# Cosine attention, Fourier mix and feed-forward on one core: a planner with new durations and new step orders

## The chip, the core and the metric

The kernel runs on one core of a Trainium2 chip. Its engines work side by side, each through its own list of instructions: TensorE (PE; loading the weights of a product is shown apart, as PEld), VectorE (DVE), ScalarE (ACT), GpSimd (POOL) and SyncE (SP), which here only issues transfers. They wait for each other by semaphores. The metric is the time of one execution on the device in microseconds (us); the median of three runs is given. One further execution was taken with the hardware profiler, and all views come from it.

## What is computed

```python
q_n = q / (norm(q, axis=-1) + 1e-6);  k_n = k / (norm(k, axis=-1) + 1e-6)
attn = softmax(q_n @ k_n.T / tau)            # 8 batches, 12 heads, 448 rows, 64 wide
x = (attn @ v) as (8, 448, 768)              # the 12 heads side by side
u = x + real(fft(fft(x, axis=1), axis=2))
un = (u - mean(u)) / sqrt(var(u) + 1e-6)     # over the 768
out = u + maximum(un @ w_ch1, 0) @ w_ch2     # 768 -> 3072 -> 768
```

## The kernel before

**Work and names.** The eight batches (0 to 7) go through the same stages, and a step's name carries the batch behind the underscore: `un0_2` is block 0 of batch 2. Where one name is given to several steps, `#1` is the second of them.

- Loads (`ld_q0_4`, `ld_k0_4`: SyncE, lines 890 and 1011; `ld_v...`: GpSimd, line 1065; the weights `W1_..` and `W2_..`: GpSimd, lines 816 and 817).
- Normalizing q and k: squares on ScalarE (`sq`, L896 for batches 0 and 1, else L1020), sums on VectorE (`ss`, L899, L1022), the reciprocal norm through logarithm and exponential on ScalarE and a reciprocal on VectorE (`ln`, `nrm`, `eps`, `rcp`: L835 to L839), scaling (`sc`). For batches 0 and 1 the scaling is `scK`, `scQ` and `scT` (L918, L922) on VectorE or GpSimd, and TensorE transposes (`tk`, `tq`); from batch 2 on it is `sc0` to `sc6` (L1033, three instructions each) on GpSimd, and transposing transfers of SyncE bring the blocks into place (`tr0` to `tr6`, L1039).
- Attention: scores on TensorE (`qk`, L1112, L1125), exponentials on ScalarE (`ex`, L1089, 900 columns an instruction), the product with v (`pv`, L1143, L1149), the reciprocal sum and the scaling on VectorE (`rd`, `x`: L1167, L1169), then small sums (`f`, `fa`, `g`, `e`).
- Fourier mix: two short products on TensorE (`fs`, `fd`), sums on VectorE (`pq` L1398, `u` L1409 or L1421), and the normalization of each block of 128 rows: `ba` (VectorE, L1446), `bs`, `ln2` and `rs` (ScalarE, L1451 to L1456), `un` (VectorE, L1463), then the transpose of the normalized block into UNT: by TensorE in batch 0 (`tn`, L1472), by a SyncE transfer from batch 1 on (`tru`, L1483, from buffer F).
- Feed-forward: products with w_ch1 (`h0` to `h23`, L1548 for the first, else L1557; two blocks together where they are a pair, `#1` for the second pair of a batch), the relu on ScalarE or VectorE (`relu`, L1573), and the products with w_ch2. These are in part formed from sums of quarters (`s10`, `s50` and such: VectorE, L1805; products `y`, `m10`, `m50`: L1701), and are put together in OUTB: by VectorE (`fin`, L1738), or by a copy on ScalarE and an addition of u on GpSimd (`fa0`, L1722, and `fa0p`, L1727, two instructions). `m50_4` accumulates on after `fin00_4`, a VectorE step that adds to what `fa0p_4` left.
- Stores: `st` on SyncE (L1752), `sc_1` and such on GpSimd (L1760).

Ahead of the first feed-forward product stand tables built on the chip (cosines and sines: `iota`, `tqs`, `sins`, `sind`, `sinp`, `sinn`, the last two being sign-changed copies for the Fourier products), the table load of ScalarE for logarithm and exponential (`ldt0`, L791), and attention and Fourier mix of batch 0. TensorE fills its pauses there with products whose result isn't used (`warm`, L1965). From the first product of line 1548 (`h0_0`) on, TensorE has work of several batches interleaved: feed-forward of one batch, attention of the next.

**What sets the order.** The program is written as a list of steps (`P.add`: the engines that may take it, a function that issues it, a duration for each engine, a name, what it reads and writes). A long string, `STEPS`, gives each step its engine and its place in that engine's list: `un0_2 326d` is the 326th place on VectorE; the letters are t (TensorE), a (ScalarE), d (VectorE), p (GpSimd), s (SyncE). A step of several instructions under one name has several numbers. SyncE's places order its transfers, and GpSimd's places its arithmetic and its transfers in one list. So the order on every engine is fixed by hand or by a search, and an engine waits at the head of its list until that step's inputs are there.

`schedule()` then walks through these lists with durations from two tables, `TIMES` (for a step and engine: time to the result, time to the next step) and `FLOW` (for a transfer: latency, service, share of the bandwidth), and with durations written at the step. What comes of this walk in the program is the slot in TensorE's accumulators (two of kind M, three of kind G) that each tile takes, and with it whom a step waits for, and the places of the warm-up products (`fill`). The steps' order comes from `STEPS` alone. `emit()` writes each engine's list with its waits.

```python
if e == "sp":
    rt = max(rt, sync[-2].end - DMA_LAT if sync[-2] else 0.0)
...
if e == "pool" and op.piece:
    port.append((t, op, op.piece))
elif e == "dve" and op.port and port and port[-1][1].end > t:
    x, p, z = port[-1]
    y = x + z * math.ceil((t - x + 0.02) / z)
    if y < p.end - 0.1:
        p.end += d
        free["pool"] += d
```

The first lines hold a transfer of SyncE in the walk until the one before the last is near its end. The others model a VectorE step (one named in `PORT`: `un`, `s`, `u`, `sc`, `f`, `g`, `e` and others) that begins while a GpSimd step made of pieces runs: the VectorE step begins at a piece's end, and the GpSimd step ends later by its duration. `QUEUES` fixes the order of the first loads.

Of the kernel before, what the change touches and what calls it, by code (L numbers as in the profile page):

```python
# [90 lines left out]
scT0_0 21d, tk0_0 0t, ek0_0 12a, tq0_0 1t, eq0_0 14a, tt0_0 3t, et0_0 27d 29, ld_k1_0 6s, ld_q1_0 0s, ld_t1_0 5s, sqK1_0 15a, ssK1_0 26d, sqQ1_0 10a,
ssQ1_0 20d, sqT1_0 13a, ssT1_0 25d, scK1_0 33d, scQ1_0 34d, scT1_0 32d, scK2_0 22p, scQ2_0 35d, scT2_0 21p, tk1_0 6t, ek1_0 36d, tq1_0 7t, eq1_0 22a,
tk2_0 13t, ek2_0 45d, tq2_0 11t, eq2_0 39d, tt1_0 10t, et1_0 43d 40, ld_k2_0 8s, ld_q2_0 4s, ld_t2_0 7s, sqK2_0 21a, ssK2_0 37d, sqQ2_0 11a,
ssQ2_0 23d, sqT2_0 24a, ssT2_0 38d, scK3_0 46d, scQ3_0 26p, scT3_0 44d, scK4_0 32p, scQ4_0 31p, scT4_0 49d, scK5_0 50d, scQ5_0 53d, scT5_0 25p,
# [1931 lines left out]
```

## Time and profile before

| | us |
|---|---|
| median of 3 runs | 573.87 (573.54 to 575.36) |
| the profiled execution | 577.4 |
| its span, first to last instruction | 575.3 |
| start of the first product of `h0_0` | 47.57 |
| TensorE busy, of the span | 555.4 |

The profiled execution lies 3.5 us above the median, and 2.1 us of it lie around its span. In the views, times are microseconds from the span's start, unless ns stands with them. A row of the timeline has start, duration, engine, line, operation, result and inputs, and the number of instructions taken together; a row of the chain of waits has start, duration and what the end was waiting for at that time. "SPq" is SyncE's issuing of a transfer, "DMA UNT<-F" the transfer itself until it has landed. Mean granted clock of TensorE over the span: 0.994.

### The profile page before, as it was taken

The numbers are of one execution on the slowest core, as the hardware profiler recorded it, in microseconds if no ns is written. First come the engines' busy times: TensorE is split into PE (matmuls) and PEld (weight loads), VectorE is DVE, ScalarE is ACT, GpSimd is POOL, SyncE is SP. The second block draws the span as 40 slices with busy tenths as digits, with TensorE's granted clock in tenths as the row PEclk, the third lists the DMA queues.
The fourth block names the chain that finished last, engine by engine and source line by source line (L and its number), as shares of the span: only waits on it lengthen the run. The fifth ranks groups of instructions, "written<-read, shape, count | busy, mean of one in ns | idle before, by whom it ended". The sixth has DMA issues, their size and how long they took to land.

```text
span 575.3 us, 15949 instructions
## 1 busy us (share of the span) xinstructions
PE 555.4 (97%) x6582; PEld 435.9 (76%) x6582; DVE 428.6 (75%) x941; ACT 368.0 (64%) x710; POOL 232.9 (40%) x346
## 2 busy tenths in 40 slices
PE   3999999999999799999999999899999999999997
PEld 2778887685786688868878788587786886969694
DVE  6989778876588468876789578876687499896362
ACT  6898885465876486787538776575566642747150
POOL 6663422367445424563471446530553103031203
PEclk9999999999999799999999999999999999999999
DMA  9999987949569936953594549634565310022011
GB/s 204 187 241 184 182 148 97 174 102 181 143 79 104 186 70 113 111 116 112 105 124 110 107 98 137 111 83 98 84 118 43 70 16 26 33 42 71 2 57 56
DMA packets 187897, 62.19 MB, mean 108 GB/s; under 512 B 166800, under 2 KB 185616, under 8 KB 187824
## 3 DMA queue, kind: packets, MB, share of 16 engines
q1 hardware_dynamic: 129856, 38.35, 35.3%
q0 software_dynamic: 57968, 22.81, 31.2%
q8 instruction: 52, 0.85, 0.6%
q14 instruction: 21, 0.17, 0.1%
HBM read 51.90 MB, written 11.01 MB: 109 GB/s over the span
## 4 chain that ended last, share of the span: by engine, by line
PE 84%; DVE 8%; POOL 3%; ACT 2%; issue 1%; DMA 1%; SPq 0%; DVEq 0%; POOLq 0%; ACTq 0%
PE PS L1557 30%; PE PS L1701 28%; PE PS L1652 7%; PE PS L1149 6%; PE PS L1112 6%; POOL QH L1033 3%; PE PS L1143 2%; PE PS L1125 2%; DVE SM L899 1%; DMA UNT<-F 1%; DVE U L1409 1%; PE PS L1310 1%; PE PS L957 1%; PE PS L1367 1%; DVE QH L922 1%
## 5 line engine op out<-in xcount | busy, mean ns | idle before, releaser
L1557 PE MATMUL PS<-UNT,W1b 128*128 128x256 bf16 (+1 forms) x1704 | 187.5, 267 | 3.4 <-DMA UNT<-F 2.8
L1557 PEld LDWEIGHTS PS<-UNT,W1b 128*128 128x128 bf16 x1704 | 154.2, 99 | 23.9 <-DMA UNT<-F 3.2
L1089 ACT ACTIVATE E<-PS 128x900 bf16<-128x900 f32 (+1 forms) x184 | 144.0, 828 | 36.7 <-PE PS L1112 29.3
L1701 PE MATMUL PS<-W2b,HQ 128*128 128x384 bf16 x720 | 126.8, 326 | 0.0
L1033 POOL TENSOR_TENSOR QH<-STG,SM 128x256 bf16<-128x256 f32 x126 | 88.3, 727 | 91.9 <-DVE SM L839 88.5
L1727 POOL TENSOR_TENSOR OUTB<-OUTB,U 128x192 f32<-128x192 f32 x72 | 47.9, 685 | 143.9 <-ACT OUTB L1722 140.7
L1701 PEld LDWEIGHTS PS<-W2b,HQ 128*128 128x128 bf16 x720 | 68.0, 98 | 42.5 <-issue 0.6
L1701 PE MATMUL PS<-TX,HQ 128*128 128x384 bf16 (+2 forms) x444 | 76.2, 322 | 2.4 <-DVE OUTB L1738 2.4
L1573 ACT ACTIVATE HQ<-PS 128x512 bf16<-128x512 f32 x76 | 45.2, 596 | 39.0 <-PE PS L1557 38.7
L1701 PEld LDWEIGHTS PS<-TX,HQ 128*128 128x128 bf16 x444 | 41.8, 98 | 29.3 <-DVE OUTB L1738 3.6
L1022 DVE TENSOR_REDUCE SM<-QH 128x6 f32<-128x384 f32 x84 | 45.2, 547 | 20.1 <-ACT QH L1020 19.6
L1805 DVE TENSOR_TENSOR HQ<-HQ 128x1536 bf16<-128x1536 bf16 (+1 forms) x73 | 51.2, 705 | 6.1 <-PE PS L1701 3.5
L1573 DVE TENSOR_SCALAR HQ<-PS 128x512 bf16<-128x512 f32 x50 | 34.2, 685 | 22.2 <-PE PS L1557 21.6
L1149 PE MATMUL PS<-VB,E 128*128 128x65 bf16 x1104 | 49.8, 193 | 0.0
L1020 ACT ACTIVATE QH<-STG 128x384 f32<-128x384 f32 x84 | 42.9, 522 | 10.0 <-DVE SM L1022 8.9
L1149 PEld LDWEIGHTS PS<-VB,E 128*128 128x128 bf16 x1104 | 46.0, 97 | 1.6
L1722 ACT ACTIVATE OUTB<-PS 128x384 f32<-128x384 f32 x36 | 17.6, 490 | 36.3 <-PE PS L1701 36.0
L1143 PE MATMUL PS<-VZ,E 128*128 128x130 bf16 x184 | 40.3, 219 | 0.0
L1112 PE MATMUL PS<-QK 64*128 64x225 bf16 (+2 forms) x864 | 40.1, 229 | 0.0
L1409 DVE SCALAR_TENSOR_TENSOR U<-ACG,X 128x768 bf16<-128x768 f32 (+4 forms) x39 | 39.6, 1022 | 0.6
L1451 ACT ACTIVATE F<-U,MV 128x768 bf16<-128x768 bf16 x28 | 26.1, 931 | 17.3 <-DVE MV L1446 13.7
L1065 POOL DMA_DIRECT2D VB<-in_v_dram x24 | 25.4, 1067 | 26.7 <-PE PS L1149 22.9
(210 smaller groups left out, 791.1 us busy)
## 6 DMA issues: line engine op xcount, KB each, us to landing
STG<-in_k_dram SPq DMA_DIRECT2D x18, 384.0 KB, 4.0
STG<-in_q_dram SPq DMA_DIRECT2D x18, 384.0 KB, 4.1
VB<-in_v_dram POOLq DMA_DIRECT2D x24, 192.0 KB, 6.7
W1b<-in_moe_w_ch_dram POOLq DMA_DIRECT2D x12, 384.0 KB, 9.7
W2b<-in_moe_w_ch_dram POOLq DMA_DIRECT2D x12, 384.0 KB, 7.7
out_dram<-OUTB SPq DMA_DIRECT2D x7, 384.0 KB, 3.2
W2b<-in_q_dram SPq DMA_DIRECT2D x2, 576.0 KB, 11.8
W2b<-in_k_dram SPq DMA_DIRECT2D x2, 576.0 KB, 11.2
```

The source lines that it names most:

```text
L1022: P.add("dve", lambda v, o=SS[:, i, H // ns * x:H // ns * (x + 1)], sq=sq: v.tensor_reduce(o, sq.rearrange("p (h d) -> p h d", d=DH), AX.X ...
L1033: r = v.tensor_tensor(v3(qh)[:, h:h + 4], v3(buf)[:, h:h + 4], RN[:, i, h:h + 4].unsqueeze(2).to_broadcast((128, 4, DH)), AluOp.mult)
L1089: return a.activation(o, self.PS[:, bk:bk + nc_, 0:SQ2], ACTF.Exp, scale=1.0 / self.tau)
L1112: i = pe.matmul(self.PS[:, bk + h, c0:c0 + n], self.KT[r, jj, kt * 128:(kt + 1) * 128], self.QT[r, jj, cols], start=True, stop=True)
L1143: r = pe.matmul(o, st(6), self.VZ[:, j, :], start=not split, stop=(split and i == 0), skip_group_check=True)
L1149: r = pe.matmul(o[:, 65 * h:65 * h + 65], st(2 * kt + h), self.VB[:, kt, 2 * j + h, :], start=(split and i == h == kt == 0), stop=((not sp ...
L1409: self.snu.append(P.add("dve", lambda v: v.scalar_tensor_tensor(two(U[o0:o0 + n, ut, :]), src, 1.0, two(X[i0:i0 + n, x, :]), AluOp.mult, A ...
L1557: r = pe.matmul(self.PS[:, bk, x * n:(x + 1) * n], self.W1b[:, j, ft * 128:(ft + 1) * 128], self.UNT[:, j, cs], start=(j == 0), stop=(j == ...
L1573: return e.activation(o, i, ACTF.Relu) if e is self.nc.scalar else e.tensor_relu(o, i)
L1701: r = pe.matmul(self.PS[:, bk, 0:n], lhs(f), rhs(f), start=(start and f == 0), stop=(stop and f == NF // 2 - 1), skip_group_check=True)
L1727: r = g.tensor_tensor(self.OUTB[:, ob, xs], self.OUTB[:, ob, xs], self.U[:, ut, xs], AluOp.add)
L1805: P.add("dve", lambda v: v.tensor_tensor(cs(o), cs(a), cs(bq), op), 0.16 + 0.3 * len(ks), -0.5, f"{nm}{ks[0]}_{b}", reads=rd, writes=[x fo ...
```

## The change

No instruction's arithmetic changes, and no step is added or left out. Four things do:

1. The tables `FLOW` and `TIMES` get new numbers, some step kinds get their own entries, and the durations written at SyncE's loads and transposes change (0.36 us per transfer to 0.5 for one and 1.35 for two; 1.45 to 1.25).
2. In `schedule()`, a GpSimd step made of pieces that begins while VectorE's last step is one of `PORT` is held until that step has ended, but for 0.14 us.
3. In `schedule()`, a transfer of SyncE waits in the walk for the fourth before it instead of the second (four open loads).
4. `STEPS` is new throughout. 62 of its 2844 steps change engine (28 from VectorE to ScalarE, 23 back, 6 from GpSimd to VectorE, 5 the other way), and many move on their own engine.

```diff
-FLOW = {r"ld_[kq]0_0": (2.47, 0.64, 1.34), r"ld_t0_0": (2.08, 0.2, 0.53), ...
+FLOW = {r"ld_[kq]0_0": (2.4, 0.1, 1.32), r"ld_t0_0": (1.87, 0.1, 0.53), ...
...
-        r"tru\d_\d": (1.81, 1.0, 0.2), ...
+        r"tru\d_\d": (2.0, 1.1, 0.2), ...
 TIMES = {
...
-        "bs1.12": (1.018, 0.919), ...
+        "bs1.12": (0.93, 0.83), ...
-        "cst0.40": (0.167, 0.187), "fap1.07": (1.234, 1.254), "fmp1.07": (1.061, 1.081), ...
+        "cst0.40": (0.25, 0.27), "fap1.07": (1.055, 1.075), "fmp1.07": (1.055, 1.075), ...
...
-        flow, now, sync, last = {"sp": [], "pool": []}, 0.0, [None, None], 0
+        flow, now, sync, last = {"sp": [], "pool": []}, 0.0, [None] * 4, 0
...
-                        rt = max(rt, sync[-2].end - DMA_LAT if sync[-2] else 0.0)
+                        rt = max(rt, sync[-4].end - DMA_LAT if sync[-4] else 0.0)
...
             if e == "pool" and op.piece:
+                if self.order["dve"] and self.order["dve"][-1].port:
+                    d += max(0.0, free["dve"] - t - 0.14)
                 port.append((t, op, op.piece))
...
-                self.loads.append(P.add("sp", fn, 0.36 * len(dm), ...
+                self.loads.append(P.add("sp", fn, 0.5 if len(dm) == 1 else 1.35, ...
```

Of `STEPS`, the places that are spoken of below (a number is the place on the engine of the letter; several numbers belong to several instructions of the name):

| step | before | after | | step | before | after |
|---|---|---|---|---|---|---|
| `sqT0_0` | 6a | 3a | | `un0_2` | 326d | 322d |
| `sqQ0_0`, `sqK0_0` | 4a, 5a | 4a, 5a | | `u1_2`, first | 324d | 326d |
| `ldt0` | 3a | 6a | | `tr5_3` | 49s | 49s |
| `scK0_0` | 14p | 21d | | `tru0_2` | 51s | 50s |
| `scQ0_0` | 19d | 20d | | `ld_q0_4` | 50s | 51s |
| `scT0_0` | 21d | 19d | | `sc5_6` | 149p | 148p |
| `et0_0` | 27d 29 | 16a 17 | | `fa0p_4` | 151p | 149p |
| `sinn` | 28d | 34p | | `sc6_6` | 150p | 150p |
| `scT1_0`, `scK3_0`, `scQ5_0` | 32d, 46d, 53d | 18p, 24p, 26p | | `un1_2`, `un2_2` | 334d, 345d | 354d, 356d |
| `scT2_0`, `scQ3_0`, `scT5_0` | 21p, 26p, 25p | 33d, 45d, 49d | | `tru1_2`, `tru2_2` | 53s, 57s | 57s, 56s |
| `W1_0` | 18p | 17p | | `un0_4` | 521d | 543d |
| `fa0p_1` | 79p | 78p | | `tru0_4` | 90s | 94s |

On ScalarE the order at the beginning was `sins sind ldt0 sqQ0 sqK0 sqT0 half ln0`, and is `sins sind sqT0 sqQ0 sqK0 ldt0 ln0`. On VectorE ahead of `un0_2` it was `pq0_2 pq0_2 eps3 rcp3 u0_2 fin20_1 ss0_4 u0_2 ss0_4 ba0_2 pq1_2 pq1_2 s40_1 u1_2 eps4 un0_2`, and is `eps3 rcp3 pq0_2 ktd3 pq0_2 fin20_1 u0_2 ba0_2 u0_2 pq1_2 pq1_2 s40_1 un0_2 ss0_4 fin31_1 ss0_4 u1_2`. On SyncE `tr3_3 tr6_3 tr5_3 ld_q0_4 tru0_2` becomes `tr3_3 tr6_3 tr4_3 tr5_3 tru0_2 ld_q0_4`.

More of the change, by code (lines that the diff above doesn't have):

```diff
@@ L91 @@
[L91 to L94, printed above, removed]
@@ L147 @@
-m52_1 304t 305 306, fm2_1 245a, fm2p_1 95p, m72_1 307t 308 309, fin31_1 327d, m32_1 310t 311 312, fin21_1 332d, sc_2_1 101p, m42_1 313t 314 316,
-fin30_1 333d, sc_3_1 99p, fd0_2 296t, qe0_2 234a, pq0_2 312d 311, u0_2 318d 315, fd1_2 298t, qe1_2 238a, pq1_2 322d 321, u1_2 324d 330 339,
-u224_2 328d, ba0_2 320d, bs0_2 242a, ln20_2 244a, rs0_2 247a, un0_2 326d, tru0_2 51s, ba1_2 329d, bs1_2 248a, ln21_2 249a, rs1_2 251a, un1_2 334d,
-tru1_2 53s, ba2_2 331d, bs2_2 250a, ln22_2 255a, rs2_2 263a, un2_2 345d, tru2_2 57s, ld_t3_3 28s, sq0_3 176a 179, ss0_3 244d 247, ln3 180a 193 211 236,
@@ L151 @@
-nrm3 183a 194 213 237, eps3 253d 260 281 313, rcp3 254d 262 284 314, sc0_3 83p, tr0_3 43s, ld_q0_3 33s, sq1_3 184a 186, ss1_3 250d 256, ld_k0_3 35s,
-sq2_3 189a 191, ss2_3 255d 257, sc1_3 84p, tr1_3 45s, sc2_3 85p, tr2_3 41s, ld_q1_3 37s, sq3_3 202a 207, ss3_3 269d 274, ld_k1_3 38s, sq4_3 205a 208,
-ss4_3 270d 273, sc3_3 87p, tr3_3 47s, sc4_3 88p, tr4_3 44s, ld_q2_3 40s, sq5_3 212a 218, ss5_3 283d 287, ld_k2_3 42s, sq6_3 229a 232, ss6_3 307d 310,
-sc5_3 94p, tr5_3 49s, sc6_3 93p, tr6_3 48s, ktd3 305d 235a, qdup3 96p, ld_v0_3 91p, ld_v1_3 89p, ld_v2_3 90p, ld_v3_3 98p, qk00_3 315t,
@@ new lines @@
+fin10_1 261d, sc_1_1 85p, m12_1 291t 292 295, fa2p_1 92p, m22_1 296t 298 299, fin20_1 315d, m62_1 300t 301 302, fv2_1 238a, fv2p_1 97p,
+m52_1 303t 305 306, fm2_1 245a, fm2p_1 96p, m72_1 307t 308 309, fin31_1 324d, m32_1 310t 311 312, fin21_1 327d, sc_2_1 101p, m42_1 313t 314 316,
+fin30_1 331d, sc_3_1 102p, fd0_2 297t, qe0_2 237a, pq0_2 314d 312, u0_2 316d 318, fd1_2 304t, qe1_2 240a, pq1_2 320d 319, u1_2 326d 330 333,
+u224_2 328d, ba0_2 317d, bs0_2 241a, ln20_2 242a, rs0_2 243a, un0_2 322d, tru0_2 50s, ba1_2 329d, bs1_2 252a, ln21_2 265a, rs1_2 273a, un1_2 354d,
@@ new lines @@
+tru1_2 57s, ba2_2 332d, bs2_2 255a, ln22_2 261a, rs2_2 277a, un2_2 356d, tru2_2 56s, ld_t3_3 28s, sq0_3 176a 178, ss0_3 244d 245, ln3 181a 195 213 235,
+nrm3 183a 196 214 236, eps3 250d 262 279 310, rcp3 252d 263 281 311, sc0_3 82p, tr0_3 43s, ld_q0_3 32s, sq1_3 185a 191, ss1_3 251d 257, ld_k0_3 34s,
+sq2_3 190a 193, ss2_3 256d 260, sc1_3 83p, tr1_3 45s, sc2_3 84p, tr2_3 41s, ld_q1_3 37s, sq3_3 205a 208, ss3_3 269d 274, ld_k1_3 39s, sq4_3 207a 210,
+ss4_3 273d 276, sc3_3 86p, tr3_3 46s, sc4_3 87p, tr4_3 48s, ld_q2_3 40s, sq5_3 212a 224, ss5_3 283d 297, ld_k2_3 42s, sq6_3 230a 231, ss6_3 305d 308,
@@ new lines @@
+sc5_3 94p, tr5_3 49s, sc6_3 93p, tr6_3 47s, ktd3 313d 244a, qdup3 95p, ld_v0_3 89p, ld_v1_3 90p, ld_v2_3 88p, ld_v3_3 91p, qk00_3 315t,
+ex0_3 249a 250 248 253, qk0t_3 324t, pv00_3 337t, pv01_3 338t, rd0_3 344d, x0_3 345d, qk10_3 329t, ex1_3 262a 259 257 266, qk1t_3 339t, pv10_3 349t,
+pv11_3 350t, rd1_3 350d, x1_3 351d, qk20_3 345t, ex2_3 269a 268 270 271, qk2t_3 351t, pv20_3 358t, pv21_3 360t, rd2_3 358d, x2_3 359d, qk30_3 354t,
+ex3_3 278a 274 275 280, qk3t_3 359t, pv30_3 367t, pv31_3 368t, rd3_3 367d, x3_3 368d, fa0_3 370d 371 374a, f00_3 372d, f10_3 373d, qk50_3 364t,
@@ new lines @@
+fd0_4 499t, qe0_4 384a, pq0_4 501d 500, u0_4 504d 503, fd1_4 506t, qe1_4 388a, pq1_4 508d 507, u1_4 510d 515 518 519, u224_4 512d, ba0_4 511d,
+bs0_4 394a, ln20_4 406a, rs0_4 425a, un0_4 543d, tru0_4 94s, ba1_4 513d, bs1_4 395a, ln21_4 398a, rs1_4 405a, un1_4 524d, tru1_4 89s, ba2_4 516d,
+bs2_4 397a, ln22_4 401a, rs2_4 416a, un2_4 534d, tru2_4 93s, ld_t3_5 60s, sq0_5 299a 308, ss0_5 395d 409, ln5 316a 339 362 380, nrm5 317a 340 363 381,
+eps5 414d 439 457 495, rcp5 416d 441 460 496, sc0_5 113p, tr0_5 80s, ld_q0_5 67s, sq1_5 331a 333, ss1_5 430d 435, ld_k0_5 69s, sq2_5 326a 336,
@@ L889, in fn @@
                         sy.dma_start(dst, src).then_inc(sem, 16)
[L890 removed]
+                self.loads.append(P.add("sp", fn, 0.5 if len(dm) == 1 else 1.35, pg[g], f"ld_{nm}{g}_{b}", writes=[f"S{nm}{g}_{b}"],
                                         dma=(f"lh{g}{nm}{b}", 16 * len(dm)), serve=sv, after=gate))
@@ L1011, in fn @@
                         sy.dma_start(dst, src).then_inc(sem, 16)
-                self.loads.append(P.add("sp", fn, 0.36 * len(dm), pr, f"ld_{kind}{t}_{b}", writes=bn,
+                self.loads.append(P.add("sp", fn, 0.5 if len(dm) == 1 else 1.35, pr, f"ld_{kind}{t}_{b}", writes=bn,
                                         dma=(key, 16 * len(dm)), after=gate, serve=1.75))
```

353 lines of the change are left out of this document (173 added, 180 removed), and 28 rows, old and new, of the table TIMES.

## The prediction

> **What bounds the kernel now.** I read the page first, the engine shares and the clock of the 40 slices, to see whether one engine carries the span.
>
> ```profile
> PE 555.4 (97%) x6582; PEld 435.9 (76%) x6582; DVE 428.6 (75%) x941; ACT 368.0 (64%) x710; POOL 232.9 (40%) x346
> PEclk9999999999999799999999999999999999999999
> ```
>
> TensorE is busy nearly throughout, and one slice only (187 to 201 us) has a lower clock. So two questions are left: what TensorE waits for, and when its stream of products begins. The view of waits of TensorE answers the first (us in total, times, longest):
>
> ```profile
> PE PS L1557 <- DMA UNT<-F: 2.8, 1, 2.8
> PE PS L1701 <- DVE OUTB L1738: 2.4, 3, 1.7
> ```
>
> Windows around these two places, with one from ahead of the stream (start and end, length, busy us of PE, PEld, DVE, ACT and POOL, then the granted clock):
>
> ```profile
> 30.00:40.00 10.00, 9.84 (x176) 7.29 (x172) 8.50 (x26) 9.79 (x14) 6.67 (x10) 1.00 1.26 246
> 191.00:194.00 3.00, 0.18 (x3) 0.09 (x3) 1.08 (x3) 3.00 (x8) 1.30 (x3) 0.85 1.37 135
> 194.00:200.00 6.00, 6.00 (x57) 5.93 (x58) 1.15 (x2) 1.23 (x3) 2.58 (x4) 0.51 0.98 259
> 362.00:365.00 3.00, 1.31 (x9) 0.60 (x7) 1.49 (x4) 0.90 (x2) 2.71 (x6) 1.00 1.11 169
> ```
>
> The reader is to see three things. At 191 TensorE stands 2.8 us and then runs six at a clock of 0.51: 6 x (1 - 0.51) = 2.9 us more are lost behind the wait. At 362 it stands 1.7 us and the clock stays at 1.00, so that wait costs only itself. And from 30 to 40 ScalarE is full (9.79 of 10): ahead of the stream not TensorE sets the time, whose busy time there holds warm-up matmuls. The stream begins here:
>
> ```profile
> 47.57 0.61 PE L1548 MATMUL PS<-UNT,W1b 128*128 128x128 bf16 x8 [0.40 <-issue]
> ```
>
> **The pause at 191.** The chain of waits (start, us, what) tells what h0_2 waited for:
>
> ```profile
> 178.60 0.94 DVE ACG L1398 x2
> ...
> 180.09 3.01 POOL QH L1033 x3
> ...
> 183.23 2.48 POOL QH L1033 x3
> ...
> 185.79 1.21 SPq L1039
> ...
> 188.03 5.84 DMA UNT<-F
> ```
>
> VectorE does pq0_2 (two instructions, 0.94) and then the reciprocal rcp3 that releases GpSimd, GpSimd scales two blocks (sc6_3, sc5_3), SyncE issues the second one's transpose (tr5_3, 185.79), the load ld_q0_4, and only at 188.03 tru0_2, the transpose that h0_2 needs; it lands after 5.84 us. Beside it, from the timeline of VectorE and of ScalarE, and the landing time of all 24 tru transposes:
>
> ```profile
> 184.01 1.22 DVE L1805 TENSOR_TENSOR HQ<-HQ 128x1536 bf16<-128x1536 bf16 x1
> 185.15 1.36 DVE L1409 SCALAR_TENSOR_TENSOR U<-ACG,X 97x768 bf16<-97x768 f32 x1
> ```
> ```profile
> 186.87 0.78 DVE L1463 TENSOR_SCALAR F<-U,MV 128x768 bf16<-128x768 bf16 x1
> ```
> ```profile
> 184.98 0.19 ACT L1456 ACTIVATE MV<-MV 128x1 f32<-128x1 f32 x1
> ```
> ```profile
> DMA to landing us min/median/max: 2.7/3.6/7.6
> ```
>
> un0_2 (186.87, done 187.65) makes tru0_2's input; the last thing that it needs itself (rs0_2, ScalarE) was there at 185.17. The change moves three things. rcp3 goes ahead of pq0_2: sc6_3, sc5_3 and tr5_3 come 0.94 earlier, tr5_3's issue ends at 185.79 + 1.21 - 0.94 = 186.1. un0_2 goes ahead of u1_2 (the 1.36), directly behind s40: 184.01 + 1.22 = 185.23, and 0.78 more is 186.0. And ld_q0_4 goes behind tru0_2. So tru0_2 is issued near 186.1, 1.9 us earlier. Landing after the median 3.6 it is there at 189.7, before TensorE stops at 191.1; after this run's 5.84, at 191.9, and the pause is 0.8. I take 0.3, between these and nearer the median, because no load is issued directly ahead any more; a pause of 1.7 drew no fall of the clock, so the fall goes too. **Gain 2.8 - 0.3 + 2.9 = 5.4** (bounds: 1.9, the shift alone with the fall kept, and 5.7). u1_2 comes about 0.8 later and feeds the next two blocks; ld_q0_4 comes about 1.2 later than right behind tr5_3 (the transpose's issue) and feeds the next batch; pq0_2 waits 0.5 for eps3 and rcp3: at nothing, and about 1 at most if the cover of the next blocks is gone.
>
> **The pause at 362.** Its chain:
>
> ```profile
> 359.05 3.64 POOL QH L1033 x3
> ...
> 362.82 1.06 POOL OUTB L1727 x2
> ```
>
> fa0p_4 (L1727, 1.06 us), whose result VectorE adds to before m50_4 may run, waits on GpSimd behind sc6_6 (3.64). The change puts it ahead of sc6_6, so 3.6 us earlier, more than the wait. **Gain 1.7** (0 to 1.7). sc6_6 and its transpose come 1.1 later; what they feed is not due while TensorE is busy with this batch's products, and if it were, the price is at most that 1.1. The other two waits of L1701 (2.4 - 1.7 = 0.7 together) are smaller ones at the same line; of them I take 0.3.
>
> **The time ahead of the stream.** Its chain, from the ACT table load on (short pieces between left out):
>
> ```profile
> 6.61 1.28 ACT L791
> ...
> 7.90 0.53 ACT HQ L896
> ...
> 9.70 0.32 ACT SM L835
> ...
> 10.84 1.23 DVE QH L922
> 12.07 0.86 DVE SM L899
> 12.93 0.21 DVE TX L918
> ```
>
> The three squares (384, 384 and 128 wide: 0.53 x 2 1/3 = 1.2) move ahead of the table load, and their reductions lie under it: the logarithm can start at 6.61 + 1.2 + 1.28 = 9.1 instead of 9.70, 0.6 earlier. Behind the reciprocal scT0, scQ0 and scK0 come first, with the reduction (0.86) after them, and scK0 leaves GpSimd for VectorE, beside which scQ0 took 1.23. At VectorE's price for an instruction of 384 that has nothing beside it (0.53, taken from the square of that width; bounds 0.4 and 1.23) the three take 0.21 + 2 x 0.53 = 1.3 instead of 1.23 + 0.86 + 0.21 = 2.3: 1.0 earlier, 1.6 together. Against that, ScalarE takes two small copies (et0) ahead of the exponentials and keeps its full stretch behind them, and VectorE gives off about as many small steps as it takes. So at 47.57 I take **1.2** of the 1.6 (-0.5 to 2.5). One large step is new on GpSimd, sinn, 900 elements; the nearest row:
>
> ```profile
> 32.67 2.15 POOL L795 TENSOR_SCALAR CS<-TX 128x770 bf16<-128x770 bf16 x1
> ```
>
> 2.15 x 900/770 = 2.5, or 3.7 if it is slowed as sc6_6 is against sc5_3 (3.64 to 2.48). It is wanted near the end of ScalarE's stretch, and GpSimd is busy 6.67 of 10 there: at nothing, and up to 3.7 if late. The W1 loads move up on GpSimd's queue: at nothing, GpSimd has room, and they were there in time before.
>
> **The rest.** Neighbouring products swap places on TensorE, and 62 of 2844 steps change engine: at nothing in the stream, where TensorE hardly waits otherwise. The planner's own edits (GpSimd held, four loads, durations) run no instruction; they alter accumulator slots and warm-up matmuls at most. But slack is spent. Two such places, each with the row it hangs on:
>
> ```profile
> 210.43 0.69 DVE L1169 TENSOR_TENSOR X<-PS,RD 128x512 bf16<-128x512 f32 x1
> ```
> ```profile
> 220.57 1.47 PE L1557 MATMUL PS<-UNT,W1b 128*128 128x256 bf16 x12
> ```
> ```profile
> 331.19 0.69 DVE L1169 TENSOR_TENSOR X<-PS,RD 128x512 bf16<-128x512 f32 x1
> ```
> ```profile
> 336.82 0.93 PE L1557 MATMUL PS<-UNT,W1b 128*128 128x256 bf16 x7
> ```
>
> un1_2 and un2_2 move behind x1_3 (210.43) and s50, so un1_2 starts near 210.43 + 0.69 + 1.22 = 212.3, un2_2 is done near 213.9 (two of 0.78), tru2_2 is issued first and tru1_2 at 213.9 + 1.21 = 215.1, wanted at 220.57: cover 5.5. un0_4 moves to where x2_5 starts now (331.19), tru0_4 is issued near 331.19 + 0.78 = 332.0, wanted at 336.82: cover 4.8. Both beat the median landing of 3.6 and miss the longest, 7.6. For these and for places that I do not see I add **1.0** (0 to 8).
>
> **Sum.** 577.4 (the profiled execution) - 5.4 - 1.7 - 0.3 - 1.2 + 1.0 = 569.8. The median of the runs, 573.87, is 3.5 below that execution. This surplus may sit in the pause at 191, whose transpose landed 2.2 us behind the median one and drew the clock's 2.9 with it (then 569.8 stands), or lie everywhere (then 569.8 - 3.5 = 566.3). I put a good third of it everywhere: 569.8 - 1.3 = **568.5**.
>
> [...]
>
> **Rivals.** (1) The pause at 191 stays. sc6_3 and sc5_3 took 3.01 and 2.48, sc6_6 3.64; if both take 3.64, beside other VectorE steps than now, tr5_3 is issued 1.8 later than worked out above and tru0_2 at 187.9, where it was: 568.5 + 5.4 = 573.9. For it: tr5_3 stays ahead of tru0_2. Against: both would have to be at the slowest that these rows show, and no load lies ahead. [...]
>
> (2) Slower: late transposes make new pauses, each with its fall of the clock. Beyond covers of 4.8 (h0_4) and 5.5 (h0_2's pair) it decides; at 7.6 each, TensorE stands 2.8 and 2.1 us: 568.5 - 1.0 + 4.9 + 2 x 2.9 = 578.2. For it: both were moved behind other steps. Against: the median is 3.6, and one place alone (568.5 - 1.0 + 5.7 = 573.2) doesn't bring it above before.
>
> (3) The start gains nothing: 568.5 + 1.2 = 569.7, and 573.4 with sinn's 3.7 on the path. For it: ScalarE is full from 30 to 40 whatever starts earlier. Against: what it waits for at the beginning comes earlier.
>
> (4) The new order takes back at unseen places what it wins: 573.9. For it: nearly every place changed. Against: the stream has 97% of TensorE now, so the waits named are nearly all there is.
>
> **Chances.** Forecast 0.68, (1) 0.08, (2) 0.08, (3) 0.10, (4) 0.06. 0.3%, or 1.7 us, is about what a measurement of this kernel can tell from no change: faster is under 572.2, slower over 575.6. Faster: 0.68 + most of (3), 0.08, + 0.02 of (1) and (4) = 0.78. Slower: (2) and 0.01 of (4) = 0.09. The same: 0.13. The range: from 566.3 less 1.3 (the start's upper bound) less 1.0 (no new wait) = 564.0 to 573.5, which takes in (3) and one late transpose and leaves out (1), (2) and (4), 2 in 10.
>
> **What would show it.** Right: no slice of the clock under 9, the wait of L1557 for UNT under 1.2, that of L1701 under 1.0, the first L1548 near 46.4, sc5_3 under 2.7. Wrong: a wait of L1557 for UNT near 221 or 337, a clock slice under 9 there, the first L1548 later than 47.6, or many small waits that sum to over 5 us.

## The result, and the profile after

| | before | after |
|---|---|---|
| median, us | 573.87 (5 runs, 573.2 to 575.36) | 569.56 (5 runs, 569.19 to 571.37) |
| ratio to before, 95% interval | | 0.9932 (0.9908 to 0.9956) |
| profiled execution, us | 577.4 | 569.29 |
| its span, us | 575.3 | 567.4 |
| start of the first product of `h0_0`, us | 47.57 | 48.11 |

The change takes 4.3 us off the median, 0.7%. The forecast was 568.5, with a range of 564.0 to 573.5. Every execution is some 2 us longer than its span (577.4 to 575.3, 569.29 to 567.4), so the time around the span is no part of the 3.5 us by which the profiled execution of before lies above its median. Every line of the new kernel from line 491 on stands two further down: L1557 is now L1559, L1701 is L1703, L1033 is L1035.

The clock's slices of the page of the changed kernel, and its view of waits of TensorE from 48 us to the end:

```profile
PEclk9999999999999999999999999999999999999999
```
```profile
PE PS L1550 <- ACT UNT L1482: 0.4, 1, 0.4
PE PS L1703 <- ACT HQ L1575: 0.3, 1, 0.3
PE PS L959 <- DVE UNT L1482: 0.2, 1, 0.2
PE PS L1559 <- DMA UNT<-F: 0.2, 1, 0.2
```

No slice is under 9. The wait for UNT (line 1557 before, 1559 now) is down from 2.8 to 0.2 us, and that of line 1701 for VectorE's OUTB (2.4 in three waits) is gone; the 0.3 of line 1703 is another, for ScalarE. In the stream TensorE hardly waits for anything. Windows of the changed kernel at the place of the old pause:

```profile
191.00:194.00 3.00, 3.00 (x56) 2.89 (x54) 2.20 (x8) 3.00 (x8) 0.91 (x2) 1.00 0.17 28
194.00:200.00 6.00, 6.00 (x116) 5.61 (x114) 5.56 (x12) 5.96 (x14) 1.26 (x3) 1.00 0.31 70
```

TensorE is busy in all 9 us, at a clock of 1.00. The table follows the same products through three executions: the profiled one of before, a second one of the same kernel (`b_copy`, below), and the changed one. Times are starts in us. Up to each of these products TensorE has done the same products in all three, warm-up products aside.

| product | before | before, second execution | after | won against the second, since the row above |
|---|---|---|---|---|
| `h0_0` | 47.57 | 47.59 | 48.11 | -0.5 |
| `m50_1` | 137.52 | 137.49 | 136.79 | 1.2 |
| `h0_2` | 193.91 | 192.79 | 189.90 | 2.2 |
| `m50_4` | 364.52 | 361.14 | 356.39 | 1.9 |
| end of the span | 575.3 | 572.0 | 567.4 | -0.2 |

So the gain comes from three stretches of the stream, and the time ahead of the stream gave a little back. The table also shows where the first profiled execution lost its 3.5 us: between `m50_1` and `m50_4`, that is at the pause and the slow clock behind it, and nowhere else.

### The profile page after: what moved, and what is told of

Read it like the earlier page. It is cut to its first block, busy times and chain, and to the rows that moved or that the text cites. A ratio compares the mean times of both kernels' runs of the same rounds, so it can differ in the third digit from the quotient of the medians.

```text
span 567.4 us, 15924 instructions
## 1 busy us (share of the span) xinstructions
PE 549.0 (97%) x6570; PEld 431.1 (76%) x6570; DVE 428.1 (75%) x937; ACT 369.2 (65%) x715; POOL 225.1 (40%) x345
## 4 chain that ended last, share of the span: by engine, by line
PE 88%; DVE 6%; DMA 2%; ACT 2%; SPq 1%; issue 1%; POOL 0%; DVEq 0%; ACTq 0%; POOLq 0%
PE PS L1703 34%; PE PS L1559 29%; PE PS L1654 7%; PE PS L1151 6%; PE PS L1114 5%; PE PS L1145 2%; PE PS L1127 2%; DMA TX<-in_k_dram 1%; DVE SM L901 1%; PE PS L1369 1%; PE PS L1312 1%; DVE U L1423 1%; SPq L891 1%; DMA UNT<-F 1%; PE PS L1308 1%
## 5 line engine op out<-in xcount | busy, mean ns | idle before, releaser
L1559 PE MATMUL PS<-UNT,W1b 128*128 128x256 bf16 (+1 forms) x1704 | 184.5, 264 | 0.2 <-DMA UNT<-F 0.2
L1559 PEld LDWEIGHTS PS<-UNT,W1b 128*128 128x128 bf16 x1704 | 152.1, 98 | 19.9 <-issue 2.0
L1703 PE MATMUL PS<-W2b,HQ 128*128 128x384 bf16 x720 | 126.3, 326 | 0.4 <-ACT HQ L1575 0.3
L1035 POOL TENSOR_TENSOR QH<-STG,SM 128x256 bf16<-128x256 f32 x126 | 83.2, 687 | 84.4 <-DVE SM L841 65.4
L1703 PEld LDWEIGHTS PS<-W2b,HQ 128*128 128x128 bf16 x720 | 68.1, 98 | 43.1 <-ACT HQ L1575 0.6
L1729 POOL TENSOR_TENSOR OUTB<-OUTB,U 128x192 f32<-128x192 f32 x72 | 43.5, 625 | 128.0 <-ACT OUTB L1724 113.1
L1703 PE MATMUL PS<-TX,HQ 128*128 128x384 bf16 (+2 forms) x444 | 76.2, 322 | 0.0
L1703 PEld LDWEIGHTS PS<-TX,HQ 128*128 128x128 bf16 x444 | 41.9, 98 | 26.3 <-issue 0.4
L1022 ACT ACTIVATE QH<-STG 128x384 f32<-128x384 f32 x84 | 43.0, 522 | 8.9 <-DVE SM L1024 7.2
L1762 POOL DMA_INDIRECT out_dram<-OUTB,IDX x21 | 23.1, 1099 | 57.7 <-DVE OUTB L1740 22.7
L1411 DVE SCALAR_TENSOR_TENSOR U<-ACG,X 128x768 bf16<-128x768 f32 (+4 forms) x39 | 38.1, 985 | 0.6
L1740 DVE TENSOR_TENSOR OUTB<-PS,OUTB 128x384 f32<-128x384 f32 x36 | 19.7, 548 | 24.8 <-POOL OUTB L1729 14.6
```

Source lines behind the costliest of these rows:

```text
L1022: P.add("act", lambda a, sq=sq, src=buf[:, w * x:w * x + w]: a.activation(sq, src, ACTF.Square), t_act(w), pr, f"sq{i}_{b}", reads=bn, wri ...
L1035: r = v.tensor_tensor(v3(qh)[:, h:h + 4], v3(buf)[:, h:h + 4], RN[:, i, h:h + 4].unsqueeze(2).to_broadcast((128, 4, DH)), AluOp.mult)
L1559: r = pe.matmul(self.PS[:, bk, x * n:(x + 1) * n], self.W1b[:, j, ft * 128:(ft + 1) * 128], self.UNT[:, j, cs], start=(j == 0), stop=(j == ...
L1703: r = pe.matmul(self.PS[:, bk, 0:n], lhs(f), rhs(f), start=(start and f == 0), stop=(stop and f == NF // 2 - 1), skip_group_check=True)
L1729: r = g.tensor_tensor(self.OUTB[:, ob, xs], self.OUTB[:, ob, xs], self.U[:, ut, xs], AluOp.add)
```

## The experiments

A place with a fraction (`323.5d`) puts a step between two others. All edits of places are made by a small table beside the reading of `STEPS`:

```diff
-            op.prio, e = plan[op.name][k]
+            op.prio, e = moved.get((op.name, k), plan[op.name][k])
```

Below, only the entries of `moved` are shown. The runs of before beside the experiments had medians of 574.53, 573.62, 574.49 and 574.25 us, in four sets. A ratio need not be that of the two medians.

### The kernel before, unchanged

> The kernel before once more, unchanged, for a second profile of it. If the pause at h0_2 belongs to the order of the steps, it is there again: TensorE waits 1.5 to 3 us for UNT near 191, and the surplus of the profiled execution over the median (3.5 us the first time) follows its size and whether the clock falls behind it. If it was an accident of one execution, the wait is under 0.5 us and the span some 5 us shorter. The wait at 362 (1.7 us) is there in both cases.

Ratio 0.9985 (0.9956 to 1.0014), span of the profiled execution 572.0. Its windows:

```profile
191.00:194.00 3.00, 1.23 (x23) 1.21 (x23) 1.08 (x3) 3.00 (x8) 1.32 (x2) 1.00 1.07 161
194.00:200.00 6.00, 6.00 (x117) 5.70 (x115) 4.12 (x8) 4.12 (x9) 2.52 (x4) 1.00 1.11 236
```

and two lines of its waits of TensorE from 48 us on:

```profile
PE PS L1701 <- DVE OUTB L1738: 2.4, 3, 1.7
PE PS L1557 <- DMA UNT<-F: 1.8, 1, 1.8
```

The pause is there again, so it belongs to the order of the steps; but it is 1.8 us and the clock stays at 1.00. The price of the place is 1.8 us in this execution and was 5.7 in the first (2.8 and 2.9). The difference, 3.9, is the whole surplus of 3.5 us of that execution over the median, within the accuracy of such a sum.

The executions without a view tell how often this happens, since the mean granted clock is known for each. Of 87 executions of before (these and the ones beside the experiments) 30 had a clock of 0.993 to 0.997 and a median of 576.3 us; the other 57, at 0.999 or 1.00, had 573.4. So about every third execution of before loses clock, and its median is taken over both kinds. Of the 43 executions of the four kernels below in which the order at `h0_2` is mended, none is under 0.999; of the 12 of `b_fa0p`, where it is not, 3 are. That shows that the fall belongs to this pause.

### Three moves at `h0_2`

```diff
+        moved = {('eps3', 3): (310.3, 'd'), ('rcp3', 3): (310.6, 'd'),
+                 ('un0_2', 0): (323.5, 'd'), ('ld_q0_4', 0): (51.5, 's')}
```

> Before, with only three moves: eps3 and rcp3 ahead of pq0_2, un0_2 ahead of u1_2, ld_q0_4 behind tru0_2. My theory (the pause at 191 is made by these orders): tru0_2 issued near 186.1, pause under 0.5 us, no fall of the clock, 3 to 5.5 us off the profiled execution and 2 to 5 us off the median. Rival (the gain of the change lies elsewhere, or the transpose's landing time decides and not its issue): pause over 2 us, median within 1 us of before.

Ratio 0.9957 (0.9936 to 0.9978), median 572.54 beside 574.53: 2.0 us. But tru0_2 was issued at 187.53, not near 186.1. The timeline of VectorE, and that of TensorE behind it:

```profile
186.50 0.54 DVE L1463 TENSOR_SCALAR F<-U,MV 128x768 bf16<-128x768 bf16 x1 [0.32 <-ACT MV L1456]
```
```profile
188.28 1.17 PE L1969 MATMUL PS<-W1b 128*128 128x128 bf16 x18
```

The first row says in its bracket that VectorE stood idle for 0.32 us until ScalarE's rs0_2 (L1456) was there. rcp3 came at 179.42, only 0.2 earlier than the 179.62 of the second execution of before, since its input too comes from ScalarE: VectorE stood idle for 0.70 us ahead of eps3. That idle time is also why rs0_2 was late: u0_2, now behind rcp3 and pq0_2, came at 180.64 instead of 179.84, ba0_2 at 184.25 instead of 183.55, and ScalarE's bs0_2 waited 0.74 us for ba0_2. The second row is new: the walk took the place for idle and put three warm-up products in, 18 matmuls, 1.0 us of TensorE's time. They fill the pause, so the wait for UNT is gone, but part of the gain went into them.

### The whole local order at `h0_2`, with and without the load's move

```diff
+        moved = {('eps3', 3): (310.3, 'd'), ('rcp3', 3): (310.6, 'd'), ('un0_2', 0): (323.5, 'd'),
+                 ('sq6_3', 1): (229.5, 'a'), ('ln3', 3): (233.3, 'a'), ('nrm3', 3): (233.6, 'a'),
+                 ('fm2_1', 0): (247.2, 'a'), ('ktd3', 1): (247.4, 'a'), ('ln4', 0): (247.6, 'a'),
+                 ('nrm4', 0): (247.8, 'a'), ('ld_q0_4', 0): (51.5, 's')}
...
-        self.P.fill(first, self.est - 20.0, self.id_op, warm(self.W1b[:, 0, 0:128]), 0.75)
+        self.P.fill(first, self.est - 20.0, self.id_op, warm(self.W1b[:, 0, 0:128]), 0.0)
```

> Before, with the local order of the changed kernel around h0_2 on all three engines: the three moves of the first try (eps3 and rcp3 ahead of pq0_2, un0_2 ahead of u1_2, ld_q0_4 behind tru0_2) and now ScalarE's too (second sq6_3 ahead of te1_2, ln3 and nrm3 ahead of qe0_2, ktd3, fm2_1, ln4 and nrm4 behind rs0_2); and without warm-up products in the stream, of which the walk had put three (1.0 us) ahead of m42_1. My theory now (the pause hung on ScalarE's order as much as on VectorE's): rcp3 near 178.0, un0_2 done near 185.5, tru0_2 issued near 185.6, no wait of TensorE for UNT, 1.5 to 2.2 us off the median. Rival (the three moves of VectorE and SyncE alone do it, and the first try only lost 1.0 us to the warm-up products): tru0_2 again near 187.5, and the gain is that of the first try plus 1.0.

> The same without the move of ld_q0_4, which stays ahead of tru0_2. If the load in front is a cost of its own, tru0_2 is issued some 0.5 us later and lands over 4.5 us after its issue instead of about 3: TensorE waits 0.5 to 1.5 us for UNT, and the median is that much longer than with the move. If not, both are equal within 0.5 us.

With the load's move: 0.9961 (0.9941 to 0.998), 572.35 beside 573.62. Without it: 0.9974 (0.9955 to 0.9994), 572.41. The timeline of SyncE, first with the move, then without:

```profile
186.76 1.42 SPq L1483 DMA_TRANSPOSE UNT<-F  x1
```
```profile
186.76 0.40 SPq L1011 DMA_DIRECT2D STG<-in_q_dram  x1
187.28 2.27 SPq L1483 DMA_TRANSPOSE UNT<-F  x1
```

TensorE no longer waits for UNT in either kernel. With the move the issue comes 0.8 us earlier than in the three moves, but 0.3 to 0.4 of that is an execution that was ahead from its start (first product at 47.16, and 47.60 without the move). Without the move un0_2 starts at 186.17 instead of 186.50 and no longer waits for ScalarE, while rcp3, at 179.43, is no earlier. So ScalarE's order has its part, some 0.3 us. Both fell short of what I expected: the issue is at 186.76 and not 185.6, rcp3 at 179.04 and 179.43 and not 178.0. The row of ln3, with the move, says why:

```profile
178.23 0.31 ACT L835 ACTIVATE SM<-SM,MV 128x24 f32<-128x24 f32 x1 [0.85 <-DVE SM L1022]
```

ScalarE stood idle for 0.85 us until VectorE's sum (L1022) was there. That sum, at 177.65, stands behind a VectorE step of line 1805 that itself waits 1.15 us for TensorE (176.78). The changed kernel has the sum ahead of that step, at 175.64.

With the load in front the transpose's issue took 2.27 us instead of 1.42 and started 0.63 us behind un0_2's end instead of 0.49, but the medians differ by 0.06 us: here it costs TensorE nothing. The changed kernel itself does better than this local order (tru0_2 is issued at 185.02), with these rows of VectorE and ScalarE:

```profile
183.60 0.95 DVE L1807 TENSOR_TENSOR HQ<-HQ 128x1536 bf16<-128x1536 bf16 x1
184.46 0.47 DVE L1465 TENSOR_SCALAR F<-U,MV 128x768 bf16<-128x768 bf16 x1
```
```profile
176.89 0.33 ACT L837 ACTIVATE SM<-SM,MV 128x24 f32<-128x24 f32 x1
177.25 0.22 ACT L839 ACTIVATE SM<-SM 128x24 f32<-128x24 f32 x1
```

ln3 is there at 176.89 against 178.70 in the first profiled execution of before: the norm's squares and logarithm were moved ahead on ScalarE, the sum on VectorE, and un0_2 follows s40 (183.60 + 0.95) at once.

### `fa0p_4` alone

```diff
+        moved = {('fa0p_4', 0): (149.5, 'p')}
```

> Before, with only fa0p_4 put ahead of sc6_6 on GpSimd. My theory: the wait of 1.7 us at 362 is gone, nothing takes its place, median 1.4 to 1.8 us shorter. Rival: sc6_6 and its transpose, 1.1 us later, make TensorE wait for qk00_6: 0.3 to 1.1 us of it come back.

Ratio 0.9973 (0.9947 to 0.9999), median 572.74 beside 574.53. Its waits of TensorE:

```profile
PE PS L1557 <- DMA UNT<-F: 2.6, 1, 2.6
PE PS L1701 <- DVE OUTB L1738: 0.7, 2, 0.5
```

The wait of 1.7 is gone and the two small ones of the same line are left; nothing was taken back by `qk00_6`. From `h0_2` to `m50_4` the profiled execution takes 166.8 us instead of the 168.4 of `b_copy`: 1.6 us. The pause at `h0_2` was not touched, and it took 2.6 us this time, with the clock at 1.00.

### Three places together

The entries of the whole local order, no warm-up products in the stream, and

```diff
+                 ('fa0p_4', 0): (149.5, 'p'), ('ld_v3_2', 0): (65.3, 'p'), ('ld_v1_2', 0): (65.6, 'p')}
```

> Before, with the three places mended together: the local order around h0_2 on all three engines as in the run before (without warm-up products in the stream), fa0p_4 ahead of sc6_6, and ld_v3_2 and ld_v1_2 early on GpSimd, which brings sc5_2 and with it fa0p_1 forward. My theory (these three places carry the whole gain of the stream, and the start gave nothing): no wait of TensorE over 0.5 us behind its first product of line 1548; 1.3 (h0_2) + 1.5 (fa0p_4) + 0.5 (fa0p_1) = 3.3 us off the median, within 0.8 us of the changed kernel's. Rival (the gain is spread over many orders): over 1.5 us behind the changed kernel.

Ratio 0.9943 (0.9922 to 0.9964), median 571.15 beside 574.49. That is 3.3 us off, the number of the sum, but 1.6 behind the changed kernel: the rival's condition, over 1.5, is met, and the theory's, within 0.8 and no wait over 0.5, is not. The waits of TensorE from 135 to 180 us:

```profile
PE PS L1143 <- issue: 0.7, 1, 0.7
PE PS L1701 <- DVE OUTB L1738: 0.5, 1, 0.5
PE PS L1364 <- ACT E L1335: 0.4, 1, 0.4
```

The second of them is the wait at `m50_1`, at 137.53 as before: the third place was not mended. The step ahead of fa0p_1 on GpSimd started at 132.68, no earlier than the 132.57 of `b_copy`, because it was waiting for VectorE's reciprocal and not for the loads:

```profile
132.68 2.93 POOL L1033 TENSOR_TENSOR QH<-STG,SM 128x256 bf16<-128x256 f32 x3 [4.04 <-DVE SM L839]
```

So it is luck that the sum of three came out. Two places were mended, and half of the 12 executions of before in this set had lost clock; against the other six (573.45) the gain is 2.3 us, and between the spans of the profiled executions 2.1 (572.0 in `b_copy`, 569.9). The last wait (0.4) goes with the second sq6_3 ahead of te1_2 on ScalarE, for it is in the two kernels with the local order too and not in before; the first (0.7) is in none of those, so it goes with the entries added here; what it waits for stays open. The changed kernel pays neither: there TensorE's own list has another product ahead of the Fourier products (m12_1 twice, then fs1_2). Where the clock holds, these two places therefore carry about half of the change's gain (2.1 of the 4.6 us between the spans), and the many small moves elsewhere carry the rest; the falls of the clock that end with the pause come on top in the median.

### The new string with the old planner

The file of before with the new `STEPS`; old tables, old `schedule()`.

> Before, with the new string STEPS and nothing else of the change (old tables, old schedule). My theory (the orders carry everything, the planner's own edits move only accumulator slots and warm-up products): the median of the changed kernel, 569.6, within 0.8 us. Rival (the held GpSimd steps and new durations matter by the slots they choose): over 571, with new waits of TensorE for an accumulator slot.

Ratio 0.9922 (0.9893 to 0.9951), median 570.97. The medians leave open whether it is slower than the changed kernel (569.56; the ratios overlap). The profile does not: its first product of line 1548 starts at 49.62, 1.5 us later than 48.11. TensorE from 13 us on, first this kernel, then the changed one:

```profile
13.17 0.50 PE L945 MATMUL PS<-TX,QH 128*128 128x128 bf16 x3
13.46 3.41 PE L1965 MATMUL PS<-TX 128*128 128x128 bf16 x30
16.80 0.58 PE L1112 MATMUL PS<-QK 64*128 64x225 bf16 x6
```
```profile
13.37 0.50 PE L947 MATMUL PS<-TX,QH 128*128 128x128 bf16 x3
13.67 1.35 PE L1967 MATMUL PS<-TX 128*128 128x128 bf16 x18
14.95 0.76 PE L1114 MATMUL PS<-QK 64*128 64x225 bf16 x12
```

Both have the same steps in the same order. The old walk thinks that the first scores come later, and puts 30 warm-up matmuls ahead of them instead of 18; TensorE takes its list in order, so the scores wait: 16.80 instead of 14.95. That is the planner's own part in the change, and it is not nothing: the theory's 0.8 us was missed (1.4 between the medians), though not by waits for accumulator slots, as the rival had it.

### The start: four tries on the changed kernel

```diff
+        moved = {('gc1_0', 1): (52.5, 'a')}
```

> The changed kernel with only gc1_0's second instruction on ScalarE put behind sqK0_1 again, where it was before. My theory (the start lost half a microsecond because sqK0_1 stands behind gc1_0, which waits 1.4 us for VectorE): sqK0_1 starts near 40.1 instead of 41.65, te0_0 0.5 earlier, the first product of line 1550 near 47.6 instead of 48.11, 0.3 to 0.6 us off the median. Rival (VectorE's own chain sets that time): first product within 0.15 us of 48.11, median unchanged.

Ratio 0.9938 (0.9917 to 0.9959), median 570.22. sqK0_1 came at 40.01 as expected, and the first product at 47.98, 0.13 earlier only: the rival. It was not ScalarE.

```diff
-            gate = [self.loads[4]] if b == 0 else [self.w[11]] if b == 1 else []
+            gate = [self.loads[4 if t == 2 else 3]] if b == 0 else [self.w[11]] if b == 1 else []
```

> The changed kernel with the loads of v (but the first) held until ld_k1_0 has landed. My theory (the loads of v, issued 3.6 us earlier than before the change, slow ld_k1_0, which lands at 13.5 instead of 11 and holds sqK1_0 and with it the second group's reciprocal): ld_k1_0 lands before 12, sqK1_0 starts 1 us earlier or more, the first product of line 1550 0.3 to 1.0 us earlier. Rival (it lands late because of the other q and k loads): ld_k1_0 lands at 13 or later, v comes later for nothing, and the first product stays or comes up to 1 us later.

Ratio 0.9918 (0.9885 to 0.995), median 569.54. The load's piece of the chain of waits is

```profile
5.63 8.03 DMA TX<-in_k_dram
```

against 7.87 in the changed kernel: it lands no earlier though the loads of v wait for it. The first product came at 48.62, 0.5 us later, with 126 warm-up matmuls ahead of it instead of 108. The rival again; why ld_k1_0 takes 2 us longer than before the change (the page of before has 5.7 for it) stays open. The first load of v, issued at 4.7 instead of 6.8, was not tried by itself.

```diff
+        moved = {('ek0_0', 0): (13.5, 'a'), ('ex0_0', 1): (17.5, 'a')}
...
-        self.P.fill(first, self.est - 20.0, self.id_op, warm(self.W1b[:, 0, 0:128]), 0.75)
+        self.P.fill(first, self.est - 20.0, self.id_op, warm(self.W1b[:, 0, 0:128]), 0.0)
```

> The changed kernel with two moves on ScalarE ahead of the stream (and no warm-up products in the stream, where it had none): ek0_0 ahead of sqK1_0, and the first exponential ahead of the second group's logarithm and norm (ln0, nrm0), behind which the change had put it. My theory (what came earlier at the start, tq0_0 by 1.3 us, was lost because ScalarE's new list holds the first exponential behind sqK1_0, which waits for a load, and behind ln0 and nrm0, which wait for a VectorE sum): the first exponential starts at 14.8 to 15.4 instead of 15.99, and the first product of line 1550 comes up to 0.8 us earlier. Rival (the time ahead of the stream is set by VectorE's full list from 24 us on, whatever the first exponential does): the first exponential comes earlier, the first product stays within 0.3 us of 48.11 and the median within 0.5 us of the changed kernel's.

Ratio 0.9917 (0.9885 to 0.9948), median 570.1. The first exponential stayed at 16.02: with ek0_0 out of the way it waited for TensorE's scores, at 15.04 behind warm-up products. The second group's reciprocal came at 17.65 instead of 16.74, and the first product at 48.73 instead of 48.11. Neither theory is right. The rows suggest that the path leads over the second group's norm, 0.9 us of which cost 0.6; one run doesn't show it.

```diff
+        moved = {('gc1_0', 1): (52.5, 'a'), ('ssK0_1', 0): (97.5, 'd')}
```

and no warm-up products in the stream.

> The changed kernel with VectorE's sum ssK0_1 (1.33 us, of batch 1) moved from ahead of u0_0 to behind un0_0, and gc1_0's second instruction behind sqK0_1. My theory (VectorE's own chain sets the first product, and this sum stands in it): u0_0 some 0.5 to 1.2 us earlier, the first product of line 1550 at 47.0 to 47.6; the median follows if batch 1's normalization, 1 us later, holds. Rival (TensorE's Fourier products set it): first product over 47.8; or the delay of batch 1 makes TensorE wait for tk0_1 or qk00_1 near 55 and takes it back.

Ratio 0.9939 (0.9914 to 0.9963), median 571.17. This one doesn't settle the start: without the sum, VectorE waited 0.61 us for TensorE's Fourier products ahead of u0_0, as the rival had it, but the walk also filled the time that it believed free with five warm-up products, directly ahead of the first product, which started at 50.14:

```profile
48.04 1.92 PE L1969 MATMUL PS<-TX 128*128 128x128 bf16 x30
50.14 0.55 PE L1550 MATMUL PS<-UNT,W1b 128*128 128x128 bf16 x7 [0.18 <-ACT UNT L1482]
```

### Few warm-up products

```diff
-        self.P.fill(max(7.5, self.id_op.end + 0.15), first, self.id_op, warm(self.ID))
+        self.P.fill(max(7.5, self.id_op.end + 0.15), 14.0, self.id_op, warm(self.ID))
```

> The changed kernel with warm-up products only up to 14 us of the walk (5 of 18 left). My theory (where the walk puts them decides 1 to 2 us of the start, as the new string with the old tables showed): TensorE's chain ahead of the first scores loses 0.5 to 1.4 us of warm-up products, the first product of line 1550 at 46.8 to 47.8, clock 1.00 throughout because no pause is over 2.6 us. Rival (they hold the clock): the granted clock falls to half somewhere between 14 and 48, the scores and transposes there take twice as long, the first product at 49 or later.

Ratio 0.9915 (0.989 to 0.994), median 569.6. Windows:

```profile
16.00:20.00 4.00, 1.99 (x20) 1.13 (x16) 3.56 (x9) 3.44 (x6) 2.41 (x4) 1.00 2.15 150
20.00:24.00 4.00, 3.73 (x44) 2.86 (x45) 3.79 (x9) 4.00 (x8) 2.47 (x4) 0.57 1.37 175
```

TensorE is busy for half of the first window, and the clock falls to 0.57 in the second, as the rival said; but the first product came at 48.45, 0.3 later, not 49 or more, and the median is the changed kernel's. The saving that the theory counted on didn't come: the first scores started at 15.61, not ahead of the 14.95 of the changed kernel, and behind 30 warm-up matmuls as there. What the fewer products and the lower clock are each worth is not told apart by this run.

None of these variants is faster than the changed kernel beyond what the intervals can tell (0.9915 to 0.9939 beside its 0.9932).

## Why the prediction was right, and where it was not

**The sum.** It was made against the profiled execution and gave 569.8; the changed kernel's profiled execution took 569.29, and its median is 569.56. That it came so near is in part luck. From the first profiled execution to the changed one the span fell by 7.9 us, of which 7.6 were forecast: 5.5 at 191 (5.4 forecast), 1.9 at 362 (1.7), 1.2 in smaller waits (0.3) and -0.5 at the start (1.2), with 0.2 lost elsewhere (1.0 allowed). The start's miss of 1.7 is covered by smaller waits that were worth more and by an allowance that was not used. The sign of being wrong that was named for the start, a first product later than 47.6, did come, and the time measured is that of rival (3), 569.7.

**The step from the profiled execution to the median** failed, by 1.3 us. I put "a good third" of the 3.5 us everywhere in the kernel. `b_copy` shows that it sat in the pause at 191 and the clock behind it alone. The sum itself was 0.2 too high, so 1.1 us are left against 568.5. Whether the executions without a profile lose clock is answered too: about one in three does (30 of 87).

**The pause at 191.** Place and mechanism were right, and the end of the wait is shown by `b_fix`: put the order right and it is gone. From `m50_1` to `m50_4` the first profiled execution took 227.0 us, the second 223.7 and the changed kernel 219.6. Of the 7.4 to the first, 1.9 belong to the pause at 362, so this place, with a wait of 0.3 at 188, gave 5.5 there (5.4 forecast); against the second execution it gave 2.2, and that is its size where the clock holds. Wrong was the list of what makes it: "three things" were named, and they brought the issue of tru0_2 to 187.53, not 186.1. rcp3's 0.94 is only 0.2, because rcp3 waits for ScalarE, and pq0_2's wait behind it, priced "at nothing", made u0_2 0.8 us later. The changed kernel, with 185.02, moves ScalarE's squares and norms and VectorE's sum as well, which I had not followed. And sc5_3, forecast under 2.7, took 3.01; sc6_3 took 1.77 instead of 3.01.

**The pause at 362.** 1.7 forecast; `b_fa0p` took 1.8 off the median and 1.6 off the stretch, and the table has 1.9. The price feared for sc6_6's transpose did not come.

**The smaller waits.** 0.3 forecast for those of L1701, where both (0.45 at 137.5, 0.29 at 188.2) are gone; 1.2 found in all from 48 to 137 us: mis-sized. Before, products there start late at 115, 118, 131 and 137 us, by 0.2, 0.4, 0.2 and 0.6 more than the product ahead takes, of which I took one kind; the view of waits lists 0.2 at 118 and 0.5 at 137.

**The time ahead of the stream** failed: 1.2 forecast, -0.5 found. What I worked out for the first group did happen (tq0_0 at 11.85 instead of 13.19). The step that failed is "VectorE gives off about as many small steps as it takes". The windows from 16 to 48 us in four parts sum up to, first before, then after:

```profile
sum 32.00, PE 30.71 PEld 24.36 DVE 29.69 ACT 27.67 POOL 18.41; mean PE 7.68 PEld 6.09 DVE 7.42 ACT 6.92 POOL 4.60
```
```profile
sum 32.00, PE 28.59 PEld 21.88 DVE 30.89 ACT 25.32 POOL 21.65; mean PE 7.15 PEld 5.47 DVE 7.72 ACT 6.33 POOL 5.41
```

ScalarE has 2.3 us less to do and is no longer full; VectorE has 1.2 us more and is at 30.9 of 32. GpSimd has 3.2 more, of which sinn is 2.46; its scaling steps are 0.9 more and stand at other times. Groups of VectorE in the same stretch, before and then after (busy us, mean ns of one):

```profile
L918 DVE TENSOR_TENSOR TX<-TX,SM 128x128 bf16<-128x128 f32 x3 | 0.8, 282 | 0.1
```
```profile
L920 DVE TENSOR_TENSOR TX<-TX,SM 128x128 bf16<-128x128 f32 x4 | 2.8, 698 | 0.0
```

The same small step of VectorE, scT, takes 698 ns instead of 282. Three of the four (at 23.6, 26.0 and 27.1 us) lie beside GpSimd's scaling steps (23.39 to 24.2 and 25.67 to 28.75), which the change has put there. In all seven profiled executions with the new string these three take 0.76 to 1.05 us, in all seven with the old one the step takes 0.27 to 0.29. The planner's rule holds GpSimd steps back in the walk; the program has no wait for it. I priced sinn's own duration on GpSimd (2.46 in the trace, 2.5 forecast) and not what VectorE's steps take beside the steps that GpSimd got. But most of this delay is made up again. Step by step, VectorE is 0.7 us behind at 28 us (27.90 instead of 27.21), 0.1 at 39.5 (39.56 instead of 39.43), and 0.5 from its next sum on (42.36 instead of 41.86) to the first product. The last 0.4 is lost in a few small steps, of which one stands for the others; before, then after, with the GpSimd step beside it, which ran at 31.12 before:

```profile
41.51 0.17 DVE L1190 TENSOR_TENSOR ACG<-ACG,F 128x4 bf16<-128x4 bf16 x1
```
```profile
41.53 0.44 DVE L1192 TENSOR_TENSOR ACG<-ACG,F 128x4 bf16<-128x4 bf16 x1
41.31 1.30 POOL L788 TENSOR_SCALAR CS<-CS,TX 128x384 bf16<-128x384 bf16 x1
```

This too is so in all seven executions of each string (0.44 and 0.17), but the order of these small steps differs a little as well. That GpSimd is the cause of the -0.5 was read from the profiles and not tried by moving the steps back.

**The allowance.** 1.0 for new waits in the stream: none came but the small ones of the view above (0.3 of L1703, 0.2 of L1559). `h0_4` and the second pair of `h0_2`, where slack was spent, show no wait; the landings of tru had a median of 2.8 and a longest of 5.7 us (3.6 and 7.6 before), and rival (2) needed 7.6. **Planner's edits "at nothing"**: right in the stream, wrong at the start, where they decide 1.5 us through the warm-up products (`b_steps`).

## What to carry to other kernels

A profile is one execution: where its time lies above the median, take a second one before pricing its biggest stall. When a wait is to be mended by reordering, follow every engine that feeds the waiting step back to what it waits for, since the list beside the obvious one may hold it. When several edits are tried at once, see in the trace that each did what it was to do before adding up their gains. And a step moved from a full engine to another is not always free (beside GpSimd's scaling steps scT took 0.76 to 1.05 us on VectorE, and 0.27 to 0.29 before): look at the mean duration of the full engine's steps, not only at their count.
